# Turning a weight block behind or ahead of the next block's maxima, in a fused threshold-attention and squared-ReLU kernel

## The chip, the core and the metric

The kernel runs on one core of one Trainium2 chip. The metric is the device time of one execution in microseconds (us); lower is better. The core's engines work side by side, each through its own queue in program order, and wait for each other on semaphores: TensorE (PE in the profile; PEld is its weight load), VectorE (DVE), ScalarE (ACT), GpSimd (POOL) and SyncE (SP), which here only issues DMAs.

## What is computed

Attention with a threshold over 8 batches and 8 heads, then a two-layer network on the result:

```python
scores = scale * np.matmul(q, k.transpose(0, 1, 3, 2))          # 8 x 8 heads, 576 x 576, head_dim 64
thresh = np.max(scores, axis=-1, keepdims=True) - tau           # tau = 0.02
scores = np.where(scores >= thresh, scores, -1000000000.0)
scores = scores - np.max(scores, axis=-1, keepdims=True)
attn = np.exp(scores)
attn = attn / (np.sum(attn, axis=-1, keepdims=True) + 1e-09)
x = np.matmul(attn, v)                                          # then (B,H,S,D) -> (4608, 512)
h = x @ w_in                                                    # 512 -> 2048
r = np.maximum(h, 0.0)
out = (r * r) @ w_out                                           # 2048 -> 512
```

All of it is in float32.

## The kernel before

**Visits, blocks and steps.** The two heads of a pair are worked on together; one pair of heads of one batch is a visit (36 visits; the first batch's four pairs are visited twice, for different rows). The 576 query rows of a visit are four whole blocks of 128 rows, numbered 0 to 3, and a rest of 64 rows, the left block, numbered 4 (`NBLK`). One block of one visit is one step; there are 148 (`NST`). From visit 12 on visits come in pairs: the even visit begins with a left block that holds the left rows of both visits, so the nine steps of a pair are left, 0, 1, 2, 3, 0, 1, 2, 3. These are the steps 40 to 147, which `late_step` (line 1065) writes out. Steps 148 to 150 have no block of their own any more; they finish what is in flight.

**A step.** At an even block or a left block TensorE computes the scores of this block and of the odd one that follows (`scores_of_two`, L296) into PSUM. Then VectorE takes the row maxima (`maxima`, L317, one for each of the two heads). ScalarE makes bias and threshold from them (`exponents`, L340 and L341) and the exponentials (L343, two). VectorE sets what lies below the threshold to zero and sums the rows (`threshold`, L355, two, then L359 and L360). POOL multiplies by the reciprocal (`divide`, L365 and L367, two). The result is the block of attention weights `w`.

**Turning.** To multiply the weights by v, TensorE needs them transposed. `turn_last(s)` (line 1050) turns the weights of step s - 1: VectorE transposes 32 x 32 squares into the tile `turned` (`turn_blocks`, L459 to L465 for a whole block, L469 for a left block). When the second block of a pair of blocks (1 or 3) is turned, `set_aside` (L436) has POOL issue a DMA of 1152 KB that copies `turned` to a buffer in DRAM, `aside`. SP later copies it back into the tile `wT` with four DMAs (`place_blocks`, L477), which puts the squares in their places; a left block goes from `turned` to `wT` by eight DMAs of SP (L486 for paired visits). SP issues the four when the copy to DRAM has landed. So the way of a block from weights to `wT` is: turn on VectorE, DMA issued by POOL, landing, four DMAs issued by SP, landing.

**Multiplying by v.** `mix` (L530) takes all blocks of a visit at once, four steps after its last block for an even visit, three for an odd one. Its first group of matmuls reads the first pair of blocks, its second group the second pair. ScalarE copies the result into `xT` (L513, L517, L524), the input of the network.

**The network.** It works through the tokens in chunks of 256. The late chunks use seven products in place of eight for each layer. Layer one (`unit`, L693, in two halves) makes seven products in the order of `UNITS`: 1 2 6 5 7 1' 3 6' 2' 4 7' 5', then 3' and 4'. Several add to the same PSUM bank: 6 adds to the bank of 1 once ScalarE has copied 1 out (L713), 7 adds to it once 6 has been copied out (L718), 3 adds to the bank of 5 (L725). VectorE adds (L705) and ScalarE squares (L701, L702). POOL and VectorE form the sums of factors for the products (L624, L670). Layer two (`product`, L799) makes seven products in fourteen half-products, with VectorE sums (L816 to L837) and POOL sums (L822, L831, and L569, L570 for `gsum`) between them.

**Order.** It is written out by hand. Each engine's instructions come in the order in which the program lists them. The pieces of the network (one unit or half-product each) are strewn between the parts of a step by `fill(quarter)`, as many as a planned rate in us allows; the plan counts pieces and does not look at the turns. `after()` lists what VectorE, ScalarE and POOL do with the pieces already listed. `some_later("gpsimd")` lists one waiting factor sum on POOL.

Where a step turns: `first` is true when the block of the step before was a block 1 or 3 or a left block. Its turn is then listed at the beginning of the step, ahead of `maxima` (L1075). When the block before was 0 or 2, its turn is listed in the middle of the step, behind `threshold` and `divide` (L1118). The last block of all (step 147, block 3 of visit 35) is turned right behind that of step 146, in the middle of step 147 (L1119). In step 147 `mix` of visit 34 and two more half-products are listed behind that place.

At the end: `mix` of visit 35 is listed at the start of step 150, and the last three chunks come behind it, as they need its result.

Of the kernel before, what the change touches and what calls it, by code (L numbers as in the profile page):

```python
# [19 lines left out]
def kernel(  # L20
# [17 lines left out]
    NBLK = S // P  # L38
# [245 lines left out]
    def area(u, odd):  # L284
        at = AT[u, odd][0]
        return big[:, at:at + S].rearrange("p (h k) -> p h k", h=2)

    def scores_of_two(s):


        vis, i = steps[s]

        def term(u, odd, second_part, lhsT, keys, to=slice(0, P)):
            at, cut = AT[u, odd]
            x0, x1 = (cut, S) if second_part else (0, cut)
            nc.tensor.matmul(big[to, at + x0:at + x1], lhsT, keys[u * D:(u + 1) * D, x0:x1], start=True, stop=True)  # L296

        if i == NBLK:
            for x in range(2):
                for v_ in range(2):  # L300
                    for u in range(2):
                        cols = slice(v_ * D, (v_ + 1) * D)
                        term(u, 0, x != u, qmid[u * D:(u + 1) * D, cols], kT[v_], cols)
            return
        for at_, (u, odd, x) in enumerate(((1, 1, 0), (0, 0, 0), (1, 0, 1), (0, 0, 1), (1, 0, 0), (0, 1, 0), (1, 1, 1), (0, 1, 1))):
            at = (i + odd) * P
            term(u, odd, x, qT[u * D:(u + 1) * D, at:at + P], kT[vis % 2])
            if at_ == 0:
                nc.scalar.copy(seen, big[:, AT[1, 1][0]:AT[1, 1][0] + 1])

    def maxima(s, sc):
        vis, i = steps[s]
        n = len(sc)
        st = stats[s % len(stats)]
        mx = st[:, 0, 0:n]
        for u in range(n):
            nc.vector.tensor_reduce(out=mx[:, u:u + 1], in_=sc[u], axis=AX.XY, op=ALU.max)  # L317
        w = w_slots[(s - first_dma) % (2 if by_dma(vis) else 3)][:, 0:n, :]
        weights[vis, i] = w, sc, st
# [17 lines left out]
    def exponents(vis, i):  # L337
        w, sc, st = weights[vis, i]
        mx, thr, bias = (st[:, j, 0:len(sc)] for j in range(3))
        nc.scalar.activation(out=bias, in_=mx, func=AF.Copy, scale=-SCALE)  # L340
        nc.scalar.activation(out=thr, in_=mx, func=AF.Identity, bias=ntau8)  # L341
        for u in range(len(sc)):
            nc.scalar.activation(out=w[:, u, :].rearrange("p (h k) -> p h k", h=2), in_=sc[u],  # L343
                                 func=AF.Exp, bias=bias[:, u:u + 1], scale=SCALE)
# [88 lines left out]
    def set_aside(vis, pair):  # L433

        t = aside[len(outside) % 4]
        nc.gpsimd.dma_start(out=t, in_=turned[:, 0:NB])  # L436
        outside[vis, pair] = t.rearrange("(b r) (j x) -> r j b x", r=32, j=4)

    def turn_blocks(vis, i):

        w = weights[vis, i][0]
        two = i < NBLK
        M = KB - 2
        if not two or i % 2 == 0:
            lo = NB if paired(vis) else NB + NB // 2
            blocks[vis, i // 2] = (turned[:, 0:NB].rearrange("p (j c u q) -> p c j u q", j=4, u=2, q=32) if two  # L450
                                   else turned[:, lo:lo + NB // 2].rearrange("p (k q) -> p k q", q=32))
        wb = blocks[vis, i // 2]
        move = nc.vector.transpose
        if two:
            wb = wb[:, :, :, i % 2, :]
            whole_, rest_ = (w[:, :, x0 * 32:x1 * 32].rearrange("p u (c j q) -> p u c j q", q=32, j=n)
                             for x0, x1, n in ((0, M, 4), (M, KB, 2)))
            h = M // 4
            move(wb[:, 0:h, :, :], whole_[:, 0, :, :, :])  # L459
            if i < 2:  # L460
                move(wb[:, h, :, :].rearrange("p (u j) q -> p u j q", u=2), rest_[:, :, 0, :, :])
            else:
                move(wb[:, h, 2:4, :], rest_[:, 0, 0, :, :])
                move(wb[:, h, 0:2, :], rest_[:, 1, 0, :, :])
            move(wb[:, h + 1:, :, :], whole_[:, 1, :, :, :])  # L465
            return
        parts = [(0, 0, KB, 0), (1, M, KB, KB), (1, 0, M, KB + 2)] if paired(vis) else [(0, 0, KB, 2), (0, M, KB, 0)]
        for u, k0, k1, at in parts:
            move(wb[:, at:at + k1 - k0, :], w[:, u, k0 * 32:k1 * 32].rearrange("p (k q) -> p k q", q=32))  # L469
# [183 lines left out]
    def some_later(engine):  # L653
        if later[engine]:
            make(*later[engine].popleft())
# [201 lines left out]
    steps = [(n, i) for n in range(len(visits)) for i in visits[n][1]]  # L857
    NST = len(steps)

    def by_dma(n):  # L860

        return n >= 3 * HP - 1
# [7 lines left out]
    for s, (n, i) in enumerate(steps):  # L870
# [5 lines left out]
        if i in mixed:  # L876
            first, lag = mixed[i]
# [38 lines left out]
    def add_chunk(j):  # L916
        waiting.extend(pieces_of(j))
        whole.add(j)
# [27 lines left out]
    def after():  # L946
        now = state["last"]
        state["last"] = []
        for fn in state["then"]:
            state["last"] += fn() or []  # L950
        state["then"] = []
        for fn in now:
            fn()

    def piece():
        _, fn, *what = waiting.popleft()
        state["left"] -= PIECE_US
        state["made"] += 1
        if fn is mlp_out or what[0] <= PLAIN and what[1] == 0:
            after()  # L960
        then = fn(*what)
        after()
        state["then"] = then
        if state["step"] >= NST:
            some_later("vector")
            some_later("gpsimd")
# [83 lines left out]
    def turn_last(s):  # L1050
        if s <= NST:
            turn_blocks(*steps[s - 1])
            n, i = steps[s - 1]
            if i % 2 and by_dma(n) and goes_out(n, i // 2):
                set_aside(n, i // 2)

    def goes_out(n, pair):

        return pair < NBLK // 2

    def at_least(count, made):
        while waiting and state["made"] < made + count:
            piece()

    def late_step(s):

        on = s < NST
        odd = on and steps[s][1] % 2 == 1
        if on:
            n, i = steps[s]  # L1070
            if not odd:
                scores_of_two(s)
            after()
        first = s > NST or steps[s - 1][1] % 2 == 1 or steps[s - 1][1] == NBLK
        if first and s != NST:  # L1075
            turn_last(s)
        if on:
            maxima(s, [area(u, odd) for u in range(2)])
            some_later("gpsimd")
            exponents(n, i)  # L1080
        valued = s in mixes and s < END

        todo = list(place_at[s])

        def place(all_):
            for what in list(todo):
                if all_ or not goes_out(*what[:2]):
                    place_blocks(*what)
                    todo.remove(what)

        if not valued:
            place(False)

        def values():
            if s in mixes:
                while (visits[mixes[s][0]][0] // HP + 1) * S - RING > read_to["x"]:
                    piece()
                mix(*mixes[s])
                for j in chunk_at.get(s, ()):
                    add_chunk(j)  # L1100

        if s == END:
            values()
        quarter = rate(s) / 4 if s < END else 1e9
        made = state["made"]
        fill(quarter)
        some_later("gpsimd")
        after()
        if on:
            threshold(n, i)  # L1110
            divide(n, i)
        if first:
            some_later("vector")
        fill(quarter)
        after()
        if not first:
            some_later("vector")
            turn_last(s)  # L1118
            if s == NST - 1:  # L1119
                turn_last(NST)  # L1120
        for fn in prep_at[s] + load_at[s]:
            fn()
        some_later("gpsimd")
        if valued:
            at_least(1, made)
            made = state["made"]
            values()
        some_loads()
        place(True)
        some_later("vector")  # L1130
        some_loads()
        fill(quarter)
        some_loads()
        fill(quarter)
        some_loads()
        if valued:
            at_least(2, made)
            state["left"] = max(state["left"], -PIECE_US / 2)
# [55 lines left out]
    for s in range(END + 1):  # L1194
# [12 lines left out]
        on = s < NST  # L1207
# [130 lines left out]
```

## Time and profile before

| what | value |
|---|---|
| time, median of 3 runs | 1348.56 us (1346.87 to 1348.89) |
| the profiled execution | 1348.56 us, its span from the first to the last instruction 1346.8 us |
| mean granted TensorE clock | 0.993 |
| TensorE busy, 0 to 210 us (first blocks, weights being prepared) | 194.57 us |
| TensorE busy, 210 to 316 us | 103.45 us |
| TensorE busy, 316 to 1100 us (784 us of late steps) | 761.97 us |
| TensorE busy, 1100 to 1175 us | 75.00 us |
| TensorE busy, 1175 us to the end | 164.93 us |
| VectorE waiting for the exponentials of ScalarE ahead of L355 | 131.5 us in 105 waits |
| VectorE waiting for scores of TensorE (L296) ahead of the maxima L317 | 19.5 us in 15 waits |
| POOL waiting for the turn on VectorE ahead of L436 | 82.4 us in 32 waits |
| copies to DRAM (L436), issue to landing | 50 of them, 4.4 to 9.8 us, median 5.1 |

How to read the lines of the profile. A row of the timeline has start and length in us, engine, line, operation, output and inputs with shape, and how many instructions it merges; in brackets, how long the engine had been idle before it and what ended the wait. A row of the waits names who waited, for whom, the total in us, how often, and the longest. SP rows are DMA issues: their length is the time of issuing, not of the transfer.

### The profile page before, as it was taken

What the parts mean: (1) busy time and instruction counts of PE and PEld (TensorE: products, weight loads), DVE (VectorE), ACT (ScalarE), POOL (GpSimd) and SP (SyncE); (2) the same over time, 40 slices, a digit from 0 to 9 for tenths busy, and PEclk for the clock granted to TensorE, in tenths of its full rate; (3) what the DMA queues carried; (4) which work ended last, traced back from release to release, by engine and by line L of the source; (5) the groups of instructions that cost most, each with busy time, mean ns of one, the idle gap of its engine ahead of it and who ended that gap; (6) DMA issues with size and microseconds to landing.
All of it is one profiled execution on the core that took longest, in us unless ns stands there. A gap on an engine that the chain in (4) does not pass through costs nothing.

```text
span 1346.8 us, 24740 instructions
## 1 busy us (share of the span) xinstructions
PE 1299.9 (97%) x8862; PEld 1076.2 (80%) x8862; DVE 942.8 (70%) x2034; ACT 582.6 (43%) x1353; POOL 777.2 (58%) x908
## 2 busy tenths in 40 slices
PE   7899999999999999999999999999999999999998
PEld 6676558787877878797978778887887888889997
DVE  6898777777778787878777757767677777632131
ACT  5887773243433534352535242524343343421321
POOL 3788875765747474656474736545464647454351
PEclk9999999999999999999999999998999999999999
DMA  6765523586778777776766657656676667520000
GB/s 125 157 180 151 132 53 90 116 199 158 173 171 164 175 163 178 174 178 149 181 172 154 150 129 147 172 126 160 155 184 133 178 143 157 157 71 1 17 17 16
DMA packets 320906, 185.47 MB, mean 138 GB/s; under 512 B 282224, under 2 KB 282256, under 8 KB 314384
## 3 DMA queue, kind: packets, MB, share of 16 engines
q1 hardware_dynamic: 309120, 115.78, 45.3%
q0 software_dynamic: 10000, 67.92, 12.7%
q8 instruction: 70, 1.15, 0.4%
q14 instruction: 52, 0.43, 0.1%
q10 hardware_dynamic: 1664, 0.21, 0.1%
HBM read 108.04 MB, written 68.42 MB: 131 GB/s over the span
## 4 chain that ended last, share of the span: by engine, by line
PE 77%; DVE 10%; ACT 4%; issue 3%; DMA 1%; POOL 1%; SPq 0%; DVEq 0%; ACTq 0%; POOLq 0%
PE big L799 28%; PE big L693 25%; PE big L530 10%; PE big L296 7%; DVE st L317 3%; PE big L579 3%; DVE w L355 2%; PE big L764 2%; PE big L280 2%; ACT w L343 2%; PE big L414 1%; POOL w L367 1%; DVE turned L465 1%; DVE gsum L823 1%; DVE gsum L624 1%
## 5 line engine op out<-in xcount | busy, mean ns | idle before, releaser
L355 DVE SCALAR_TENSOR_TENSOR w<-big,st,w 128x576 f32<-128x576 f32 x269 | 209.6, 815 | 133.5 <-ACT w L343 131.5
L367 POOL TENSOR_SCALAR w<-w,st 128x576 f32<-128x576 f32 x269 | 244.9, 919 | 30.9 <-DVE st L360 27.0
L799 PE MATMUL big<-wo,gsum 128*128 128x256 f32 x1088 | 243.8, 382 | 0.0
L799 PEld LDWEIGHTS big<-wo,gsum 128*128 128x128 f32 x1088 | 204.4, 190 | 37.0 <-issue 8.2
L317 DVE TENSOR_REDUCE st<-big 128x1 f32<-128x576 f32 x288 | 202.8, 743 | 43.9 <-PE big L280 21.4
L365 POOL TENSOR_SCALAR st<-st 128x2 f32<-128x2 f32 (+1 forms) x148 | 35.6, 241 | 289.3 <-DVE w L355 279.8
L693 PE MATMUL big<-xT,w_in_sb 128*128 128x128 f32 x1536 | 187.0, 278 | 8.2 <-ACT g L718 7.2
L693 PEld LDWEIGHTS big<-xT,w_in_sb 128*128 128x128 f32 x1536 | 179.0, 193 | 17.6 <-ACT g L718 8.6
L799 PE MATMUL big<-wo,g 128*128 128x256 f32 x816 | 185.3, 382 | 0.2 <-ACT g L701 0.2
L343 ACT ACTIVATE w<-big,st 128x576 f32<-128x576 f32 x255 | 173.9, 732 | 0.2 <-issue 0.2
L799 PEld LDWEIGHTS big<-wo,g 128*128 128x128 f32 x816 | 151.6, 190 | 26.2 <-issue 6.5
L530 PE MATMUL big<-wT,vs 128*64 128x256 f32 (+5 forms) x1420 | 159.2, 389 | 1.6 <-ACT wT L415 1.0
L340 ACT ACTIVATE st<-st 128x2 f32<-128x2 f32 (+1 forms) x137 | 27.9, 203 | 296.5 <-DVE st L317 295.5
L530 PEld LDWEIGHTS big<-wT,vs 128*64 128x64 f32 (+1 forms) x1420 | 85.1, 136 | 67.4 <-issue 16.1
L705 DVE TENSOR_TENSOR g<-big,g 128x512 f32<-128x512 f32 x96 | 65.6, 683 | 99.5 <-PE big L693 88.7
L296 PE MATMUL big<-kT,qT 64*128 64x256 f32 (+3 forms) x768 | 107.6, 416 | 0.2 <-DVE w L355 0.2
L296 PEld LDWEIGHTS big<-kT,qT 64*128 64x128 f32 x768 | 84.7, 186 | 15.2 <-issue 3.3
L569 POOL TENSOR_TENSOR gsum<-g 128x512 f32<-128x512 f32 x34 | 46.0, 1354 | 70.2 <-ACT g L702 65.2
L702 ACT ACTIVATE g<-g 128x512 f32<-128x512 f32 x128 | 80.7, 630 | 4.1
L701 ACT ACTIVATE g<-g 128x512 f32<-128x512 f32 x96 | 60.3, 628 | 49.1 <-DVE g L705 48.7
L436 POOL DMA_DIRECT2D aside<-turned x50 | 29.8, 595 | 88.9 <-DVE turned L465 82.4
L693 PE MATMUL big<-t,g 128*128 128x128 f32 x512 | 65.1, 289 | 10.7 <-ACT g L713 10.6
(119 smaller groups left out, 2073.4 us busy)
## 6 DMA issues: line engine op xcount, KB each, us to landing
aside<-turned POOLq DMA_DIRECT2D x50, 1152.0 KB, 5.1
wT<-aside SPq DMA_DIRECT2D x200, 288.0 KB, 5.1
vs<-in_v_dram SPq DMA_DIRECT2D x72, 128.0 KB, 5.8
wo<-in_moe_w_in_dram SPq DMA_DIRECT2D x16, 512.0 KB, 5.1
wo<-in_moe_w_out_dram SPq DMA_DIRECT2D x16, 512.0 KB, 3.5
out_dram<-osb POOLq DMA_DIRECT2D x32, 256.0 KB, 3.3
kl<-in_k_dram SPq DMA_DIRECT2D x113, 72.0 KB, 2.8
ql<-in_q_dram SPq DMA_DIRECT2D x112, 72.0 KB, 5.5
```

Source lines behind the costliest of these rows:

```text
L296: nc.tensor.matmul(big[to, at + x0:at + x1], lhsT, keys[u * D:(u + 1) * D, x0:x1], start=True, stop=True)
L317: nc.vector.tensor_reduce(out=mx[:, u:u + 1], in_=sc[u], axis=AX.XY, op=ALU.max)
L343: nc.scalar.activation(out=w[:, u, :].rearrange("p (h k) -> p h k", h=2), in_=sc[u], func=AF.Exp, bias=bias[:, u:u + 1], scale=SCALE)
L355: nc.vector.scalar_tensor_tensor(out=wu, in0=sc[u], scalar=thr[:, u:u + 1], in1=wu, op0=ALU.is_ge, op1=ALU.mult, accum_out=sm[:, u:u + 1])
L367: nc.gpsimd.tensor_scalar(out=w[:, u, :], in0=w[:, u, :], scalar1=z[:, u:u + 1], scalar2=rcp[:, u:u + 1], op0=ALU.add, op1=ALU.mult)
L530: nc.tensor.matmul(ps[u * D:(u + 1) * D, :], vs[n % 2][rows, u * (NBLK + 1) + c, :], wT[rows, at // REST:(at + ps.shape[1]) // REST, NBLK ...
L569: nc.gpsimd.tensor_tensor(out=gsum[0][:, f, :], in0=g[:, f, P:], in1=g[:, lo + HF:lo + HF + HF // 2, P:], op=ALU.add)
L693: nc.tensor.matmul(to[:, f, :], factor(j, p, q, c)[:, f * P:(f + 1) * P], part[:, c, :], start=(p in "125" and f == 0 and c == 0), stop=(p ...
L701: nc.scalar.activation(out=to, in_=to if src is None else src, func=AF.Relu)
L702: nc.scalar.activation(out=to, in_=to, func=AF.Square)
L705: nc.vector.tensor_tensor(out=x, in0=to, in1=x, op=ALU.add)
L799: nc.tensor.matmul(to, left[:, f, :], wo[:, slot, f, :], start=(f == 0), stop=(f == HF - 1))
```

## The change

The turns that stood at the beginning of a step are listed behind `maxima`, one factor sum and `exponents` of that step. The copy to DRAM that belongs to such a turn moves with it on POOL's queue. The turn of the last block is no longer listed in the middle of step 147, but at the beginning of step 148, ahead of that step's pieces and behind what step 147 lists after its middle. Nothing else changes: the turns of blocks 0 and 2 stay, and so does every piece of the network.

```diff
             after()
-        first = s > NST or steps[s - 1][1] % 2 == 1 or steps[s - 1][1] == NBLK
-        if first and s != NST:
-            turn_last(s)
-        if on:
             maxima(s, [area(u, odd) for u in range(2)])
             some_later("gpsimd")
             exponents(n, i)
+        first = s > NST or steps[s - 1][1] % 2 == 1 or steps[s - 1][1] == NBLK
+        if first:
+            turn_last(s)
         valued = s in mixes and s < END
...
         if not first:
             some_later("vector")
             turn_last(s)
-            if s == NST - 1:
-                turn_last(NST)
         for fn in prep_at[s] + load_at[s]:
             fn()
```

The functions it calls are these:

```python
    def turn_last(s):
        if s <= NST:
            turn_blocks(*steps[s - 1])
            n, i = steps[s - 1]
            if i % 2 and by_dma(n) and goes_out(n, i // 2):
                set_aside(n, i // 2)
    def goes_out(n, pair):
        return pair < NBLK // 2
```

## The prediction

> **What bounds the kernel.** I read the page's busy times first, then the waits of TensorE, then the timeline around the longest of them, and last the copies through DRAM.
>
> ```profile
> PE 1299.9 (97%) x8862; PEld 1076.2 (80%) x8862; DVE 942.8 (70%) x2034; ACT 582.6 (43%) x1353; POOL 777.2 (58%) x908
> ```
>
> TensorE works 97% of the span and the change leaves its instructions as they are. So a gain can come only out of its waits, and a loss is a new one. The waits of TensorE from 250 to 1175 us, which is the stage the change touches:
>
> ```profile
> PE big L693 <- ACT g L713: 12.9, 8, 3.1
> PE big L693 <- ACT g L718: 7.2, 5, 2.4
> PE big L693 <- ACT g L725: 1.9, 2, 1.5
> PE big L296 <- DVE kT L254: 1.1, 1, 1.1
> PE big L693 <- DVE g L705: 0.9, 1, 0.9
> ```
>
> These are 24 us. They are the seven products (L693) waiting for ScalarE to copy a PSUM bank out before the next product adds to it. ScalarE itself is 43% busy, so I looked at what its copy stood behind. The timeline of one such wait:
>
> ```profile
> 836.67 3.84 PE L693 MATMUL big<-xT,w_in_sb 128*128 128x128 f32 x32
> ...
> 838.06 0.38 DVE L837 TENSOR_TENSOR osb<-big,osb 128x256 f32<-128x256 f32 x1
> 838.37 0.69 DVE L459 STREAM_TRANSPOSE turned<-w 128x512 f32<-128x512 f32 x1
> 838.99 0.27 DVE L461 STREAM_TRANSPOSE turned<-w 128x128 f32<-128x128 f32 x1
> 839.18 0.67 DVE L465 STREAM_TRANSPOSE turned<-w 128x512 f32<-128x512 f32 x1
> 839.77 1.38 DVE L317 TENSOR_REDUCE st<-big 128x1 f32<-128x576 f32 x2
> ...
> 841.18 0.20 ACT L340 ACTIVATE st<-st 128x2 f32<-128x2 f32 x1 [5.77 <-DVE st L317]
> 841.29 0.28 ACT L341 ACTIVATE st<-st,ntau 128x2 f32<-128x2 f32 x1
> 841.48 1.36 ACT L343 ACTIVATE w<-big,st 128x576 f32<-128x576 f32 x2
> ...
> 842.73 0.58 ACT L713 COPY g<-big 128x512 f32<-128x512 f32 x1
> ...
> 843.46 0.77 PE L693 MATMUL big<-t,g 128*128 128x128 f32 x2 [2.96 <-ACT g L713]
> ```
>
> The reader is to see the order: turn, maxima, exponents, copy L713, product. The scores had been ready since 836.7, yet the maxima stood behind the turn until 839.77.
>
> **The change, part by part.** It neither adds nor removes work: 61 turns (five in each pair of visits, and the very last) move. Sixty go from ahead of the maxima to behind the exponents' issue, on VectorE behind the maxima; with them 47 copies to DRAM (L436) move on POOL's queue, behind one factor sum (L624, 1.3 us) where one waits. The 61st, of the last block, goes from step 147 to 148, with the 48th copy.
>
> *VectorE.* For each moved turn I took from the timeline when VectorE came free, when the scores ended and how long the turn (1.5 to 1.65 us) and the two maxima (1.38) last. The maxima now start at the later of the first two, the turn runs after them, the threshold starts when turn and first exponential (1.1 us after the maxima) are both done. In the mean over 59 steps the maxima come about 0.7 us earlier, the threshold 0.3 earlier, the turn 2.4 later (1.3 where the scores were ready, up to 4.7 where they were not). VectorE's 1.09 us before L355, idle in nearly every step, takes the turn in; that is the cover, and without it the threshold would be 1.5 later.
>
> *Gain.* The waits of TensorE over 0.25 us, one by one, in time, length and what comes off:
> 843.46 (2.96): VectorE free at 838.4, maxima at 839.77, off 1.4. 991.42 (3.07): free 986.3, maxima 987.73, 1.4, of which the next copy keeps 0.2: 1.2. 915.52 (3.06): the step before had a turn at 903.12 with scores ready at 901.1; its threshold comes 1.1 earlier and VectorE has no gap from there to the maxima of the stalled step: 1.1. 769.89 and 777.23 (1.07, 2.39): the same 1.1 from the step before, then maxima 1.25 earlier: 2.3. 1060.09 to 1073.35 (three, 2.38): 1.1 twice over two steps, at most 2.2 of 2.38, taken 2.0. 282.65 and 291.73 (2.36): 1.05. 567.12 and 571.89 (1.44): 0.75. 430.91 (1.54): 0.3. 705.31 (1.02): 0.15. 500.26 and 789.55 (2.57): nothing, the maxima there waited for scores. Sum 10.25 us. Bounds: the four plainest, 1.4 + 1.2 + 1.1 + 2.3 = 6.0, and everything but the last two, 21.3.
>
> *Sums that follow.* In thirteen steps a sum (L705, L819 or L821) stands between maxima and threshold, now behind the turn. Mostly it waits for TensorE longer; at 860, 1024 and 1110 us it comes about 1 us later. Bounds 0 and 2.9, taken 0.5, as no wait of TensorE stands there now.
>
> *POOL.* L436 now waits for a turn 2.4 us later. Queued behind it: a factor sum or the two gsum sums (L569, L570), then the division, which waits for the threshold anyway, 1.96 us after the turn's end. The gsum sums come 2 to 4 us late at four places; their reader, product 5, is some three products of 3.45 us away. Cost 0.
>
> *SP.* Its queue stands on each copy's landing, with the loads of k and q behind. The least time between such a load's landing and its transpose is 8.0 us, against a shift of at most 4.7: cost 0.
>
> *Copies through DRAM.* Slack is small only at odd visits. From the landing of the last L477 to the matmul that reads it: visit 13, 1.7 us; 15, 0.25; 17, 1.8; 19, 1.4; 33, 3.2; 21 to 31, 3.5 and more. Turns there come 3.9, 2.2, 2.2, 2.2 and 4.2 later. If landings shifted as much, that is 2.2 + 1.9 + 0.4 + 0.8 + 1.0 = 6.3 us. But the copy to DRAM is not free to run: SP's four L477 of the first block pair go out just before, and land 7.7 us after their issue whether or not the copy is under way. The copy of visits 13, 15, 17, 21 and 33, issued 3.8 to 6.1 us after them, landed 12.0 to 12.2 us after them, 4.3 to 4.5 behind the last of them, though it takes 4.4 alone. Issued later it lands nearly as before: shift about 0.4, and only 15 pays, 0.2. Visit 19 landed after 10.5; there the shift is 1.9 and 0.55 is paid. Sum 0.75.
>
> [...]
>
> *The tail.* The last block's turn has no later work to hide behind:
>
> ```profile
> 1171.26 0.67 DVE L465 STREAM_TRANSPOSE turned<-w 128x512 f32<-128x512 f32 x1
> 1171.53 12.26 SPq L477 DMA_DIRECT2D wT<-aside  x8
> 1172.23 0.60 POOL L436 DMA_DIRECT2D aside<-turned  x1 [1.41 <-DVE turned L465]
> 1173.46 0.42 DVE L816 TENSOR_TENSOR osb<-big,held 128x256 f32<-128x256 f32 x1 [1.53 <-PE big L799]
> ...
> 1189.79 0.44 PE L530 MATMUL big<-wT,vs 128*64 128x256 f32 x2 [0.24 <-DMA wT<-aside]
> ```
>
> Turn, copy out (landed 1182.01), four copies back (last landed 1189.65), matmul: its slack is spent. Moved to step 148 the turn stands behind L816, which waits for TensorE until 1173.46: it ends at 1175.4, and the copy goes out at 1175.65, 3.4 later. By the rows of visits 13 and 33 it lands 12.05 after SP's 1171.53, at 1183.6: 1.6 later. Bounds: 0.1 (10.5 after, as at visit 19) and 3.4. TensorE has nothing queued that could fill it; the last three chunks stand behind. Taken 1.6.
>
> **Sum.** -10.25 + 0.5 + 0.75 + 1.6 = -7.4. The profiled run took 1348.56 us, 1.8 of them outside its span of 1346.8, and is itself the median of the runs. Span 1339.4, time 1341.2. Its own range: 1338.3 (no cost) to 1346.7 (6.0 gained, 0.75 and 3.4 paid).
>
> **Rivals.** *The copies through DRAM come late (slower).* Place: the second block pair of odd visits, and the tail. With the turn's shift in full it costs 6.3 + 3.4 = 9.7; landings also spread by 1.5 us (copies landed 2.9 to 4.5 behind SP's last), which on these six places makes 18.7 at most. Middle 14.2: -10.25 + 0.5 + 14.2 = +4.4, so 1353.0. It decides once landings shift as much as the turns. For it: these transfers are the only path whose slack is below the shift, and SP waits 222.8 us on such landings in this stage. Against it: the five landings above, and one wait of 0.2 us for them now.
>
> *The waits only move (no change).* The next copy out of PSUM has the same two microseconds' room between product and product, so TensorE may run into it. If 2.85 of the 10.25 stays, it cancels the costs: 1348.6. For it: sixteen waits in some 45 such places, whose pattern shifts with every microsecond. Against it: the exponents ahead of these copies start earlier in every step but the few that wait for scores.
>
> *The gain grows.* Earlier thresholds carry VectorE ahead over several steps. 15 of the 21.3 and none of the costs but 0.5: 1334.1.
>
> That the change does nothing is excluded: the order on VectorE is other in 61 places.
>
> **Chances.** Forecast 0.52, larger gain 0.05, no change 0.11, late copies 0.32. A measurement of this kernel can tell about 0.2%, 2.7 us. Faster 0.57, same 0.11, slower 0.32. The slower case holds too much to leave out, so the range reaches from 1336, between forecast and larger gain, to 1355, past the middle of the late copies.
>
> **What would show it.** Right: L355's idle before falls from 131.5 us to about half, L317's on TensorE's scores rises by tens of us from 19.5, "PE big L693 <- ACT g L713" falls from 12.9 to about 7, and the copies of visits 13, 15, 17 and 33 land within half a microsecond of where they did, seen from SP's issue. Wrong: rows "PE big L530 <- DMA wT<-aside" of several us, at odd visits above all; or L713 and L718 summing to 20 us as before, at other places. The tail by itself: the wait before the last L530, 0.24 now, at about 1.8.

## The result and the profile after

The changed kernel takes 1335.74 us, the median of 4 runs (1333.27 to 1338.4), against 1348.72 us of the kernel before beside it (4 runs, 1346.87 to 1349.4). The ratio is 0.9906, with a 95% interval of 0.9885 to 0.9928: about 13 us faster, where 7.4 were forecast. The profiled execution took 1335.76 us, with a span of 1334.0 us (1346.8 before) and a mean granted TensorE clock of 0.997 (0.993 before). The granted clock is the share of full speed at which the profile shows TensorE's clock; a stretch at 0.5 is called half clock below.

First the busy times of the page of the kernel after, and three of its groups of instructions (busy time and mean ns of one; then the idle time before them and what ended most of it):

```profile
PE 1294.1 (97%) x8862; PEld 1071.7 (80%) x8862; DVE 937.6 (70%) x2034; ACT 583.4 (44%) x1353; POOL 776.3 (58%) x908
```

```profile
L355 DVE SCALAR_TENSOR_TENSOR w<-big,st,w 128x576 f32<-128x576 f32 x269 | 207.8, 808 | 80.9 <-ACT w L343 78.6 <-ACT st L331 1.5
L317 DVE TENSOR_REDUCE st<-big 128x1 f32<-128x576 f32 x288 | 204.3, 748 | 97.0 <-PE big L296 70.7 <-PE big L280 22.2 <-ACT g L701 1.9
L436 POOL DMA_DIRECT2D aside<-turned x50 | 29.9, 597 | 177.1 <-DVE turned L465 177.1
```

The turn now fills VectorE's wait for the exponentials (131.5 us before, 78.6 now), and VectorE stands ready for the scores instead (19.5, now 70.7). POOL waits longer for the turn (82.4, now 177.1). TensorE's number of instructions is the same, yet its busy time is 5.8 us less than before (1299.9). That was not in the prediction, and it is nearly half of the result.

The waits of TensorE from 250 to 1165 us in the kernel after (who waited for whom, total in us, how often, longest):

```profile
PE big L693 <- ACT g L718: 6.3, 6, 1.8
PE big L693 <- ACT g L713: 6.2, 5, 1.9
PE big L530 <- DMA wT<-aside: 1.8, 2, 1.3
PE big L693 <- DVE g L705: 1.1, 1, 1.1
PE big L693 <- ACT g L725: 0.6, 1, 0.6
...
```

The wait for L713 is halved, and the odd visits' copies through DRAM (L530) are a new row. Here is the same place of the kernel after whose timeline the prediction showed (the wait of 2.96 us at 843.46):

```profile
832.26 1.40 DVE L317 TENSOR_REDUCE st<-big 128x1 f32<-128x576 f32 x2
833.59 0.68 DVE L459 STREAM_TRANSPOSE turned<-w 128x512 f32<-128x512 f32 x1
...
835.97 1.24 PE L693 MATMUL big<-t,g 128*128 128x128 f32 x9 [1.58 <-ACT g L713]
```

The maxima come first, the turn right behind them, beside the exponentials, and the product waits 1.58 us: 1.38 less.

**Where the 12.8 us of span come from.** All waits of TensorE over 0.25 us behind 210 us, called late waits below, and the tail's (0.24 us before) sum to 24.1 us before and 17.3 after: 6.8 less. The busy time is 5.8 less. Together 12.6. The busy time is less mostly because TensorE's clock was granted at half less often. Windows of TensorE behind long waits, first three of the kernel before, then one of the kernel after (stretch, length, busy time and instructions, granted clock, DMA share, GB/s):

```profile
843.00:849.00 6.00, 5.54 (x36) 0.72 0.70 277
915.00:922.00 7.00, 6.48 (x32) 0.53 1.16 228
991.00:997.00 6.00, 5.58 (x48) 1.00 0.90 304
```

```profile
905.60:911.60 6.00, 6.00 (x37) 0.72 1.14 207
```

Before, the clock goes to half within 1 us of the end of the waits of 2.39, 2.96 and 3.06 us (granted clock 0.50 from 778.16, 843.02 and 914.70), for 3.41, 3.41 and 6.83 us; around the one of 3.07 us at 991.42 it stays full (1.00 from 984 to 997 us). The 32 matmuls of a piece, 3.84 us otherwise, take 5.23 us behind the wait at 843:

```profile
843.46 5.23 PE L693 MATMUL big<-t,g 128*128 128x128 f32 x32 [2.96 <-ACT g L713]
```

TensorE was busy for 12.4 us of these stretches, so half speed cost it 6.2 by my estimate, half of that time. After, only the wait of 1.88 us at 905.56 is followed by one, of 3.41 us: 1.7. That is 4.5 of the 5.8 us; the rest I did not find in single places. The 4.5 us hold for this pair of executions and are in part the luck of the draw: the profiled execution of the run with POOL's part alone below, whose late waits of 24.6 us are much those of before, had a mean granted clock of 0.995, and that of the run with the other fifty steps 0.992, against 0.993 before.

### The profile page after: what moved, and what is told of

Its sections match the earlier page's. It is cut to its first block, busy times and chain, and to the rows that moved or that the text cites. A ratio compares the mean times of both kernels' runs of the same rounds, so it can differ in the third digit from the quotient of the medians.

```text
span 1334.0 us, 24740 instructions
## 1 busy us (share of the span) xinstructions
PE 1294.1 (97%) x8862; PEld 1071.7 (80%) x8862; DVE 937.6 (70%) x2034; ACT 583.4 (44%) x1353; POOL 776.3 (58%) x908
## 3 DMA queue, kind: packets, MB, share of 16 engines
q0 software_dynamic: 10000, 67.92, 12.6%
## 4 chain that ended last, share of the span: by engine, by line
PE 79%; DVE 8%; ACT 3%; DMA 3%; issue 2%; POOL 0%; SPq 0%; DVEq 0%; ACTq 0%; POOLq 0%
PE big L799 28%; PE big L693 25%; PE big L530 10%; PE big L296 8%; PE big L579 3%; DVE st L317 2%; PE big L764 2%; PE big L280 2%; DVE w L355 2%; DMA wT<-aside 1%; DMA aside<-turned 1%; ACT w L343 1%; PE big L414 1%; DVE turned L459 0%; DVE turned L154 0%
## 5 line engine op out<-in xcount | busy, mean ns | idle before, releaser
L317 DVE TENSOR_REDUCE st<-big 128x1 f32<-128x576 f32 x288 | 204.3, 748 | 97.0 <-PE big L296 70.7
L355 DVE SCALAR_TENSOR_TENSOR w<-big,st,w 128x576 f32<-128x576 f32 x269 | 207.8, 808 | 80.9 <-ACT w L343 78.6
L530 PE MATMUL big<-wT,vs 128*64 128x320 f32 (+5 forms) x1420 | 159.7, 389 | 4.6 <-DMA wT<-aside 3.3
L530 PEld LDWEIGHTS big<-wT,vs 128*64 128x64 f32 (+1 forms) x1420 | 85.5, 136 | 70.6 <-issue 20.8
L436 POOL DMA_DIRECT2D aside<-turned x50 | 29.9, 597 | 177.1 <-DVE turned L465 177.1
L705 DVE TENSOR_TENSOR g<-big,g 128x512 f32<-128x512 f32 x96 | 65.1, 678 | 92.7 <-PE big L693 87.1
L296 PE MATMUL big<-kT,qT 64*128 64x256 f32 (+3 forms) x768 | 106.5, 416 | 0.0
L296 PEld LDWEIGHTS big<-kT,qT 64*128 64x128 f32 x768 | 84.4, 186 | 14.3 <-issue 5.3
L701 ACT ACTIVATE g<-g 128x512 f32<-128x512 f32 x96 | 60.3, 628 | 56.7 <-DVE g L705 56.6
L702 ACT ACTIVATE g<-g 128x512 f32<-128x512 f32 x128 | 80.7, 630 | 4.1
L459 DVE STREAM_TRANSPOSE turned<-w 128x512 f32<-128x512 f32 x100 | 70.3, 703 | 0.0
```

The costliest lines, as they stand in the source:

```text
L355: nc.vector.scalar_tensor_tensor(out=wu, in0=sc[u], scalar=thr[:, u:u + 1], in1=wu, op0=ALU.is_ge, op1=ALU.mult, accum_out=sm[:, u:u + 1])
L530: nc.tensor.matmul(ps[u * D:(u + 1) * D, :], vs[n % 2][rows, u * (NBLK + 1) + c, :], wT[rows, at // REST:(at + ps.shape[1]) // REST, NBLK ...
L701: nc.scalar.activation(out=to, in_=to if src is None else src, func=AF.Relu)
L702: nc.scalar.activation(out=to, in_=to, func=AF.Square)
L705: nc.vector.tensor_tensor(out=x, in0=to, in1=x, op=ALU.add)
```

## Experiments

Each ratio is to the kernel before, run beside it on the same chip.

**The last turn back in its place.** The change without the move to step 148:

```diff
-        if first:
+        if first and s != NST:
             turn_last(s)
...
             turn_last(s)
+            if s == NST - 1:
+                turn_last(NST)
```

> The changed kernel with the last block's turn back right behind that of step 146, in step 147; the sixty other turns stay behind the maxima. Theory (the tail is the change's one fixed cost: copy to DRAM issued 3.4 us late, landing 1.2 to 1.6 us late, nothing to fill it): about 1.3 us faster than the changed kernel, near 1334.4 us, and the wait of TensorE before the second group of the last L530 falls from 1.4 us to 0.3 or less. Rival (the transfers absorb the later issue, the tail costs nothing): no difference from the changed kernel, within 0.5 us.

1334.66 us (1331.71 to 1335.22), ratio 0.9897 (0.9882 to 0.9912). The wait before the last L530 is 0.30 us against 1.44. So the move cost 1.1 us by the wait, and the medians agree. The intervals of the two ratios overlap: the cost is shown by the wait, not by the times alone.

**POOL's part alone.** Turn ahead of the maxima as before; only the copy to DRAM is listed behind the factor sum and the exponents:

```diff
         if first and s != NST:
-            turn_last(s)
+            turn_last(s, False)
         if on:
             maxima(s, [area(u, odd) for u in range(2)])
             some_later("gpsimd")
             exponents(n, i)
+        if first and s != NST:
+            copy_last(s)
```

(`copy_last` is the second half of `turn_last`, the call of `set_aside`; `False` leaves it out there.)

> The kernel before, with only POOL's order changed: turns stay ahead of the maxima on VectorE, but the copies to DRAM stand behind the factor sum. Theory (VectorE's order makes the gain: maxima, exponents and PSUM copies come earlier): no gain, 1347 to 1350 us, waits of TensorE for L713 and L718 near 20 us as before. Rival (the gain comes from POOL, which forms a factor sum instead of standing idle for the turn): most of the 13 us, 1336 to 1340 us, and those waits fall.

1347.92 us, ratio 1.0001 (0.9993 to 1.001), late waits 24.6 us: nothing.

**VectorE's part alone.** The maxima ahead of the turn, but the copy to DRAM still ahead of the factor sum on POOL, the tail as before:

```diff
+        if on:
+            maxima(s, [area(u, odd) for u in range(2)])
         if first and s != NST:
             turn_last(s)
         if on:
-            maxima(s, [area(u, odd) for u in range(2)])
             some_later("gpsimd")
             exponents(n, i)
```

> The kernel before, with only VectorE's order changed: maxima ahead of the turn, while the copy to DRAM stays ahead of the factor sum on POOL and the last turn stays in step 147. Theory: all of the gain and the tail's 1.3 us on top, 1333 to 1336 us; waits for L713 and L718 near 12 us in sum. Rival (POOL): near 1348 us; a mixture would lie between, by as much as POOL's share.

1338.13 us (1337.14 to 1338.35), ratio 0.9926 (0.9913 to 0.9938): 3.5 us behind the run with both parts and the same tail, which I had not expected. Late waits are 19.0 us against 16.0. The timeline of the place where they differ most, first of VectorE's part alone, then with both parts:

```profile
566.89 0.54 POOL L436 DMA_DIRECT2D aside<-turned  x1 [1.60 <-DVE turned L465]
...
567.45 1.28 POOL L624 TENSOR_TENSOR gsum<-w_in_sb,g 128x512 f32<-128x512 f32 x1
...
568.35 2.76 DVE L624 TENSOR_TENSOR gsum<-w_in_sb 128x512 f32<-128x512 f32 x1
569.26 1.28 POOL L624 TENSOR_TENSOR gsum<-w_in_sb,g 128x512 f32<-128x512 f32 x1
...
573.56 1.70 PE L693 MATMUL big<-xT,w_in_sb 128*128 128x128 f32 x9 [2.13 <-ACT g L718]
```

```profile
563.80 1.29 POOL L624 TENSOR_TENSOR gsum<-w_in_sb,g 128x512 f32<-128x512 f32 x1
...
565.28 0.56 POOL L436 DMA_DIRECT2D aside<-turned  x1 [0.18 <-issue]
...
566.41 1.28 POOL L624 TENSOR_TENSOR gsum<-w_in_sb,g 128x512 f32<-128x512 f32 x1
...
566.74 1.59 DVE L624 TENSOR_TENSOR gsum<-w_in_sb 128x512 f32<-128x512 f32 x1
...
570.79 2.39 PE L693 MATMUL big<-xT,w_in_sb 128*128 128x128 f32 x19 [0.97 <-ACT g L718]
```

With the copy in front, POOL stands 1.60 us at L436 until the later turn is done, and two of its factor sums (L624, 1.28 us) come after that, beside VectorE's own factor sum for 1.67 us, which then takes 2.76 us. With both parts one factor sum runs on POOL ahead of the copy, the one behind it runs beside VectorE's sum for only 0.95 us, and that takes 1.59 us. VectorE's sum starts equally long (some 0.65 us) after the start of the product's matmuls in both, so the 1.17 us that it takes longer make what follows on VectorE late, and with it L718: the wait is 1.16 us longer. This is one place of several. By the medians POOL's part is worth nothing alone and 3.5 us behind VectorE's part.

**Ten steps only.** Of the sixty moves only those of the ten steps that lie at or just ahead of a long wait:

```diff
+        behind = s in (43, 45, 79, 101, 103, 110, 117, 126, 133, 135)
+        if first and s != NST and not behind:
+            turn_last(s)
...
             exponents(n, i)
+        if behind:
+            turn_last(s)
```

> The kernel before, with the turn behind the maxima in only ten of the sixty steps, those that the forecast named as upstream of TensorE's waits (steps 43, 45, 79, 101, 103, 110, 117, 126, 133, 135); tail as before. Theory (the gain sits where VectorE was free, the scores were ready and a product waited downstream): 8 to 13 us of gain, 1336 to 1341 us. Rival (the gain is spread over all steps through VectorE's idle time before the threshold): a sixth of it, about 2 us, 1346 us.

1334.41 us (1333.44 to 1334.76), ratio 0.9899 (0.9884 to 0.9914): as much as all sixty without the tail (0.9897), and a little more than expected. Late waits are 16.0 us, with none at the odd visits' L530 but 0.31 us at the tail.

**The other fifty.** The complement of these ten, the tail as before:

```diff
+        behind = first and s < NST and s not in (43, 45, 79, 101, 103, 110, 117, 126, 133, 135)
```

> The complement of the ten steps: the other fifty turns behind, the ten and the last where they were. Theory (the gain sits in the ten steps that end in a wait of TensorE): waits before L713 and L718 stay near 20 us, two waits before L530 near 410 and 554 us come on top, time 1346 to 1350. Rival (VectorE being earlier in every step adds up over the stage): half the gain or more is here, 1337 to 1342.

1346.11 us (10 runs, 1343.8 to 1348.0), ratio 0.9988 (0.9978 to 0.9998). The waits of TensorE from 250 to 1185 us:

```profile
PE big L693 <- ACT g L713: 12.2, 6, 3.1
PE big L693 <- ACT g L718: 6.6, 5, 2.4
PE big L530 <- DMA wT<-aside: 1.8, 2, 1.3
...
```

Earlier maxima in fifty steps change little: L713 and L718 wait as in the kernel before, and the two waits before L530 come on top. VectorE's lead does not add up over the stage; it is worth what it takes off a wait in its own step or the next.

**The same waits taken away by another route.** Turns and maxima as in the kernel before; in thirteen steps the exponents alone are listed later, behind the first quarter of pieces, and so behind the copy out of PSUM on ScalarE:

```diff
-            exponents(n, i)
+            late = s in (44, 45, 62, 71, 79, 80, 95, 103, 110, 118, 126, 134, 135)
+            if not late:
+                exponents(n, i)
...
         if on:
+            if late:
+                exponents(n, i)
             threshold(n, i)
```

> The kernel before, every turn where it was; only in the thirteen steps with waits are the exponentials listed behind the first quarter of pieces. Theory (turn, maxima and exponentials cost TensorE only as far as the copy of a PSUM bank stands behind them): the waits of 2.4 to 3.1 us at 777, 843, 915 and 991 fall under 1 us without any turn moved, late waits from 24 to 10 or less, and with them the half clock behind them: 1330 to 1337. Rival (the gain comes from VectorE being earlier, by its threshold and what follows): waits stay above 18 us and the time within 2.7 us of the kernel before, 1345 to 1350.

1337.75 us (1336.92 to 1338.73), ratio 0.9928 (0.9915 to 0.9942), a little outside the expected 1330 to 1337. Late waits fall from 24 to 16.8 us, not to the expected 10, and the mean granted clock was 0.997 (1.00 from 840 to 846 and from 909 to 915 us). The place of the wait of 2.96 us in this run:

```profile
833.15 0.58 ACT L713 COPY g<-big 128x512 f32<-128x512 f32 x1 [3.34 <-PE big L693]
...
834.17 1.38 DVE L317 TENSOR_REDUCE st<-big 128x1 f32<-128x576 f32 x2
834.74 3.74 PE L693 MATMUL big<-t,g 128*128 128x128 f32 x32
```

The maxima are as late as ever, the copy runs ahead of them, and the product waits for nothing. So the wait here came from the copy of a PSUM bank being queued behind the exponents on ScalarE. The expectation failed at one of its four places: near 982 us a wait of 3.29 us came up, since there the copy L718 now stood behind squares (L701, L702) that wait for a sum of VectorE. Later exponents also cost: the next scores (L296) wait up to 1.05 us for the threshold (L355).

**Both routes in the ten steps.** The ten turns behind, and the exponents late in eleven steps:

```diff
+            late = s in (45, 62, 71, 80, 95, 103, 110, 118, 126, 127, 135)
```

> The ten turns behind, and in the eleven steps where TensorE still waits for a copy out of PSUM the two exponentials are listed on ScalarE behind the first quarter of pieces, so behind that copy. Theory (what is left of the waits is the copy standing behind 1.36 us of exponentials on ScalarE): late waits fall from 16 us to 6 or less, and the time from 1334.4 to 1325 to 1329. Rival (exponentials that start later make the threshold late, and the steps after it pay): waits turn up in the steps behind the eleven, sum 12 us or more, time 1331 to 1338.

1332.52 us (1331.15 to 1333.02), ratio 0.9886 (0.9873 to 0.99): a gain over the ten turns that the intervals don't separate, and the rival's forecast, with late waits of 12.5 us. The waits for PSUM copies at 704, 774, 837, 907 and 978 us are gone, and those near 500 and 571 us stayed. But the one at 983 grew from 0.95 to 2.83 us as above, and new ones came up as the rival had it: near 434 us the scores (L296) wait 1.05 us for the threshold (L355), in place of a wait of 1.54 for L725, and then 0.63 us for ScalarE; near 830 us they wait 0.57 us; and near 917 us a product waits 1.09 us for L713.

**Without the moves of steps 58 and 76.** These turn the second block pair of visits 15 and 19, whose copies through DRAM came late:

```diff
-        if first and s != NST:
+        if first and s != NST and s not in (58, 76):
             turn_last(s)
```

(they are listed ahead of `maxima` again).

> The sixty moved turns less the two of steps 58 and 76, whose copies to DRAM came late for the second block pair of visits 15 and 19, and the last turn in its old place. Theory (each late copy costs its own wait and nothing hides it): the two waits before L530 near 410 us (0.68 with sixty) and 554 us (1.13) fall under 0.25, and the time goes 1.5 to 2 us below the 1334.7 of the sixty without the tail, to 1332.5 to 1333.3. Rival (TensorE runs into the next copy out of PSUM instead): waits before L693 behind 410 and 554 grow by as much and the time stays at 1334 to 1335.

1329.84 us (1328.6 to 1332.78), ratio 0.9871 (0.9855 to 0.9887). Both waits (0.68 and 1.13 us) are gone. Behind the second, the wait near 571 us fell too, from 0.97 to 0.48 us; behind the first, the wait for L725 near 430 us grew from 0.49 to 1.39 us, as the rival had it for that place. Late waits are 14.1 us against 16.0. The gain in the medians, 4.8 us, is larger than that. At the same mean clock of 0.995 the two kernels took 1335.0 and 1332.78 us, at 0.998 they took 1331.71 and 1330.28: 2.2 and 1.4 apart, about what the waits are worth. But the two fastest executions (1328.6 and 1329.4 us) had 0.997, so the mean clock does not explain the rest, and where it comes from stays open; the intervals of the two ratios overlap slightly.

**The best of both.** The same fifty-eight turns, and the exponents late where the run with eleven steps had gained by it: in steps 95, 103, 110 and 118, and in a second kernel in 126 as well.

```diff
+            late = s in (95, 103, 110, 118)
```

> The fifty-eight turns behind (without steps 58, 76 and the last), and the exponentials behind the first quarter of pieces in the four steps 95, 103, 110 and 118 alone, where the run with eleven such steps lost its waits and made none. Theory (both routes take away the same kind of wait and add up where they don't meet): the waits of 0.66, 1.08, 1.58 and 1.87 us near 704, 773, 836 and 906 fall to 0.6 in sum, late waits from 14.1 to about 10, time 3.5 to 5.5 us below the 1329.8 of the fifty-eight, 1324.3 to 1326.3. Rival (later exponentials are paid in the next steps): 1329 to 1332.

> As the run with four, and step 126 as a fifth. Theory: the wait of 1.64 us near 978 goes too, and the one near 982 (0.95), which grew to 2.83 where step 127 had late exponentials as well, stays near 1: 1 to 1.8 us below the run with four. Rival (the 2.83 us came from step 126's later threshold): the wait near 982 grows to 2 us or more, and time is equal to that with four or above it.

1326.48 us (1324.32 to 1328.34), ratio 0.9838 (0.9824 to 0.9851), just above the expected 1324.3 to 1326.3, with late waits of 8.7 us (the four waits are gone); and 1326.22 us (1325.56 to 1326.48), ratio 0.9836 (0.9822 to 0.9849). These are the fastest versions, about 22 us below the kernel before and 9 below the changed one. The fifth step added nothing: its own wait of 1.64 us went, and the one behind it (0.94 us in the run with four) grew to 2.84 us, as its rival said.

**A made wait and the clock.** To the changed kernel, 8, 16, 24 and 36 copies of one column on ScalarE (0.22 us each) were added ahead of L713 in chunks 4, 6, 8 and 13:

```diff
+                elif state["step"] < NST:
+                    for _ in range({4: 8, 6: 16, 8: 24, 13: 36}.get(j, 0)):
+                        nc.scalar.copy(seen, ident[:, 0:1])
                 nc.scalar.copy(g11, to)
```

> The changed kernel, with short one-column copies put on ScalarE ahead of four of the L713 copies (8, 16, 24 and 36 of them, in chunks 4, 6, 8 and 13), to make four waits of TensorE of growing length, some 0.8 to 4 us. Nothing of the computation is left out. [...]

One execution, 1347.23 us, span 1345.4. Late waits grew by 9.6 us over the kernel after, busy time by 1.9. The made waits were 1.29, 3.08 and 7.57 us; chunk 8 showed none. In the longest, which ended at 1057.44, the clock fell to half some 2 us after TensorE had stopped, and stayed there for some 10.2 us, by the granted clocks of 0.82 from 1050 to 1053 us, 0.98 from 1062 to 1066, and 0.50 between them:

```profile
1053.00:1062.00 9.00, 4.56 (x20) 0.50 0.58 134
```

There 16 matmuls took 3.75 us, where 32 took 3.74 at 834.74 in the run with the exponents late. Behind the 3.08 us the clock stayed at full (1.00 from 568.4 to 574.4 us). So in these runs the length alone did not decide it. The wait near 498 us (1.83 us in the kernel after) shows the same. It stood, with 1.8 us, in the run with the tail back (first line) and in the run without steps 58 and 76 (second):

```profile
499.00:502.50 3.50, 3.50 (x33) 1.00 0.56 141
```

```profile
499.00:502.50 3.50, 3.50 (x21) 0.55 0.69 156
```

The same code and the same wait: 33 matmuls in 3.5 us in one, 21 in the other.

## Why the prediction was right, and short in size

**What bounds the kernel, and the mechanism: right.** The gain in waits came out of waits for PSUM copies queued on ScalarE behind the exponentials. The run with late exponents alone shows that queue to be the cause. One reading was loose: of the 24 us of waits before, 22 were for ScalarE and 2.0 for VectorE (L254 and L705). The size was short: the measured 1335.74 us lies 2.6 us under the sum's own range (1338.3 to 1346.7) and at the lower edge of the wide one (1336).

**The gain in waits: right, 9.9 us against 10.25.** Place by place, forecast and measured: 843.46: 1.4 and 1.38. 915.52: 1.1 and 1.18. 769.89 and 777.23: 2.3 and 2.38. 1060 to 1073: 2.0 and 1.91. 991.42: 1.2 and 0.5, since a second wait of 0.94 us came up behind it. 282 and 291: 1.05 and 1.7. 430.91: 0.3 and 1.0. 705.31: 0.15 and 0.4. 567 and 571: 0.75 and -0.1. 500 and 789: 0 and -0.4. Three of the four plainest fell as worked out, the one at 991.42 by less than half. The small ones are off to either side, and that they cancel is luck.

**The odd visits: undersized, 1.84 us against 0.75.** Visit 15 paid 0.58 instead of 0.2 and visit 19 paid 1.26 instead of 0.55. The step "issued later it lands nearly as before" held better than the rival of late copies (9.7 us and more): visits 13, 17 and 33 paid nothing. Counted from SP's first issue, the copies of visits 13, 15, 17 and 33 went out after 8.06 us in place of 3.8 to 5.9, and landed 0.48, 0.59, 0.51 and 0.39 us later than before, against 0.4 forecast. That of visit 19 landed 2.66 us later (after 13.18 us instead of 10.52), where 1.9 was forecast.

**The tail: 1.2 us against 1.6.** A step of the chain of waits of the kernel after (start, length):

```profile
1161.65 7.68 DMA aside<-turned
```

The copy went out 4.1 us after SP's four of 1157.53 and landed 11.8 after them, where 12.05 was forecast; the last L530 waited 1.44 us, forecast 1.8. An issue 3.4 us later than in the kernel before, counted from SP's, moved the landing by 1.3 us: this copy took 7.68 us, 9.8 before, where the shortest of the fifty before took 4.4.

**POOL, "cost 0": right for the change as made, for half of the reason.** With both parts the waits fell as forecast, and POOL's part alone does nothing. But the prediction looked only at what is queued behind L436. It did not see that the factor sum listed ahead of the copy matters as well: the run with VectorE's part alone, without it, was 3.5 us slower.

**Sums behind the turn, 0.5:** no new wait of TensorE was found there.

**What was missing: TensorE's busy time, 5.8 us, of which 4.5 were found at half clock.** In waits the change was worth 6.8 us (9.85 - 1.84 - 1.20), close to the 7.4 forecast. The sum had no term for what a long wait costs after it ends, though the mean clock of 0.993 stood in the table. The measured time is nearer to that of the rival "the gain grows" (1334.1) than to the forecast (1341.2), but not by its mechanism: the run with the other fifty steps speaks against a lead that adds up.

**The signs named.** L713 fell to 6.2 (named: about 7), L355's idle time to 60% (about half), L317's rose by 51 us, the tail came to 1.44 (about 1.8); the copies of visits 13 and 33 landed within half a microsecond of where they did, those of 15 and 17 just beyond it.

## What to carry to other kernels

Find what each short stall of the bounding engine is queued behind, on the engine that releases it, and reorder there and then only: here ten of sixty moves brought as much as all sixty, and two of the others took some of it back. Listing a PSUM copy ahead of exponentials took the same stalls away as making the exponentials earlier, and the two together made the best kernel, as long as the copy did not land behind something that waits longer. A TensorE stall of two to three us cost more than its length in three of four places of the kernel before (behind the one of 2.96 us, 32 matmuls took 5.23 us in place of 3.84); look at the granted clock behind it.

## What the runs showed of the chip that was not expected

**Behind some waits of 1.8 to 3.1 us TensorE's clock was at half, behind others at full.** Between 250 and 1170 us the trace before has three stretches at half clock, of 3.41, 3.41 and 6.83 us, and the trace after has one of 3.41. Each begins within 1 us of the end of a wait, of 2.39, 2.96 and 3.06 us before and of 1.88 after. The waits of 3.07 us at 991.42 before, of 1.83 at 497.32 after and of 3.08 in the run with made waits went with none.

The three stretches before begin 64.85 and 71.68 us apart, which is 19 and 21 times 3.413 us, the length of the two shorter ones. I counted on from the beginnings of these stretches in steps of that length, and did the same in the trace after, and laid the waits on the steps. The four waits that went with half clock had 1.88 to 2.52 us inside one step. The other waits of the two traces had at most 1.63: the 3.07 us at 991.42 falls as 1.44 and 1.63 into two steps, the 1.83 us at 497.32 as 0.92 and 0.91. In the run with made waits this fails: counted back from its half clock at about 1051.9, the 3.08 us (565.3 to 568.4) had some 1.9 us inside one step and went with none. No run moved a wait against the steps on purpose, and what decides was not shown.

**The granted clock differs from run to run of the same program.** The 15 runs of the kernel before beside the run without steps 58 and 76 go from 1345.86 us at a mean clock of 0.996 to 1349.55 at 0.991. Where their half-clock stretches lay is not shown.
